# Linformer attention with a routed expert layer: W2's casts on other engines, batch 1's queries in other buffers, exponentials as steps of their own

## The chip, the cores and the metric

The kernel runs on one core of a Trainium2 chip. A core has five engines with queues of their own, each working strictly in the order of the program: TensorE (PE; the profile lists its weight loads apart, as PEld), VectorE (DVE), ScalarE (ACT), GpSimd (POOL) and SyncE (SP), which here only issues DMAs. The metric is the device time of one execution in microseconds (us); lower is better. A time that is called the median is that of several executions; the trace and the page come from one profiled execution, which has a time of its own.

## The reference, cut to what matters

Eight batches of 8 heads, 576 tokens, head width 64, 32 memory slots. All data are 32-bit floats.

```python
a = softmax(phi, axis=2)                              # [b, h, s, 32]
k_m = einsum('bhsm,bhsd->bhmd', a, k)                 # 32 keys and values a head
v_m = einsum('bhsm,bhsd->bhmd', a, v)
attn = softmax(q @ k_m.T / 8)                         # [b, h, s, 32]
x = (attn @ v_m) as [4608, 512]                       # heads side by side

logits = unit(x) @ unit(expert_emb).T / tau           # 8 experts
e = argmax(logits)                                    # one expert a token
gate = softmax(logits)[e]
out = gate * (relu(x @ w1[e]) @ w2[e])                # w1 [512, 1024], w2 [1024, 512]
```

The kernel computes the output of a batch with the expert that most of its tokens choose; tokens of other experts, if there are any, are done over at the end.

## The kernel before, in words

The heads lie in two groups of four (`g` = 0, 1). For a batch the work is:

- *Memory* (`softmax`, `turn`, `slots`, `block`, `flip`): exponentials of phi, its transposes, 32 keys and values per head. `block` scales them out of the accumulator `acc` (VectorE for the keys, line 427; ScalarE for the values, line 428), `flip` transposes them on TensorE (line 436) and ScalarE copies them out.
- *Scores* (`scores`, `Tokens.fill`, `weigh`, `divide`, `turn`): queries against the 32 keys on TensorE (line 453), copied to the buffer `sT` by ScalarE, and then per group a softmax over 32 values in `x`, [128, 576]: VectorE transposes (line 63), takes the maximum (line 70) and subtracts it (line 72), ScalarE takes the exponential (line 73), VectorE sums, divides (line 83) and transposes into `aw` (line 89).
- *Attention and routing* (`attend`, `norm`, `count`, `choose`, `late`): the rows of x with the logits, their lengths, the batch's expert. `choose` reads the expert into SyncE and issues the loads of that expert's W1, and for batches after the first those of W2.
- *Projection* (`project`, lines 531 to 535): the values times W1, in two halves of 512 columns, so that the first layer is one product of the attention weights `aT` with `gh` and `gl`. High and low parts (`...h`, `...l`) of a 32-bit number are kept apart, and a product is three products of such parts.
- *First layer* (`first`, lines 541 to 559): 2 halves of the tokens times 8 chunks of 128 columns, 16 chunks in all; six matmuls each (line 550) into one of four accumulators of the tag `mm`, drained by ScalarE's relu (line 553), VectorE's low part (line 554) and, in the second half, a second relu by ScalarE for the half tile (line 558).
- *Second layer* (`second`, lines 561 to 598): first the half tile, 64 tokens, straight from the 32-bit W2 in `w2s` (line 572); then four full tiles of 128 tokens. A full tile is 8 row blocks of W2 (`f` = 0 to 7), each three matmuls in the order `wh` with the high part, `wl` with the high part, `wh` with the low part (line 583). All five tiles end with a scaling by the gate (line 596) and an output DMA, which GpSimd issues.

The halves of W2 are made by `split_w` (line 514), one row block of 128x512 a call: a cast of `w2s` to `wh` by ScalarE (line 518), for blocks 1 and 5 by VectorE (line 520), then `wl` = `w2s` - `wh` by GpSimd (line 521).

The order on each engine is written by hand. `steps` builds two lists: what is issued behind each of the 16 chunks of the first layer (`first[0]` to `first[15]`) and behind each step of the second (`second[0]` to `second[7]` are the half tile, `second[8]` to `second[15]` the row blocks of the first full tile, and so on). These steps hold W2's split, the rest of this batch's routing and the preparation of the next batch `c` = b + 1 (`u`) and the memory part of b + 2. `batch` runs projection, first and second layer and calls the steps in between; `must(f)` sees that block f is split before a full tile reads it. So in batches 1 to 6 blocks 0 to 3 are split behind chunks 1, 3, 5 and 11 and blocks 4 to 7 behind steps 0, 2, 4 and 6 of the half tile, while both groups' `divide` and `turn` stand at `second[0]`. In batch 0 block 0 is split behind chunk 15 and the others in the half tile.

Loads are issued in order on SyncE's queue. Batch 0's queries and, from batch 2 on, all later ones come into `qt`. Batch 1's come into the front of `w2s`, so W2 of batch 0 is loaded only behind batch 1's scores, at `first[5]` of batch 0. Ahead of the batch loop, `moe_linformer` does the memory part and the scores of batch 0, chooses its expert from the first two of five token tiles, and prepares the memory of batch 1.

## Time and profile before

| | us |
|---|---|
| median of 3 runs | 508.51 (506.0 to 509.23) |
| the profiled execution | 506.96 |
| its span, first to last instruction | 505.0 |
| TensorE busy in it | 444.5 (88%) |
| VectorE, ScalarE, GpSimd busy | 275.4, 200.2, 133.0 |
| mean granted TensorE clock | 0.939 of full speed |

A row of a group names line, engine, operation, output and inputs, partitions x elements and how often; behind the bar stand busy time and mean ns of one, then how long the engine stood idle just ahead of these instructions and what ended that. A row in order of time begins with its start and its length in us from the start of the span. SPq rows are DMA issues on SyncE's queue. A row of stretches begins with the bounds in us. Matmuls overlap in the array and their ends are modelled, so the distance between two starts says more than a length does. The granted clock is 1.00 or 0.50 at any time; a mean lies between.

### The profile page before, as it was taken

The numbers are of one execution on the slowest core, as the hardware profiler recorded it, in microseconds if no ns is written. First come the engines' busy times: TensorE is split into PE (matmuls) and PEld (weight loads), VectorE is DVE, ScalarE is ACT, GpSimd is POOL, SyncE is SP. The second block draws the span as 40 slices with busy tenths as digits, with TensorE's granted clock in tenths as the row PEclk, the third lists the DMA queues.
The fourth block names the chain that finished last, engine by engine and source line by source line (L and its number), as shares of the span: only waits on it lengthen the run. The fifth ranks groups of instructions, "written<-read, shape, count | busy, mean of one in ns | idle before, by whom it ended". The sixth has DMA issues, their size and how long they took to land. (4 is left out here: it accounts for less than half of the span.)

```text
span 505.0 us, 9258 instructions
## 1 busy us (share of the span) xinstructions
PE 444.5 (88%) x3511; PEld 349.2 (69%) x3511; DVE 275.4 (55%) x854; ACT 200.2 (40%) x515; POOL 133.0 (26%) x132
## 2 busy tenths in 40 slices
PE   4679859999799997999799997999979998899994
PEld 3548537867587865868488684877758785688783
DVE  5675772746572675735745366726656367365300
ACT  3525423265233652246422463316522355115410
POOL 1020162222530324203333124303143032433400
PEclk9759969999799998999979999999979999899998
DMA  8962921694039800696018830298104800175011
GB/s 311 344 217 56 354 96 51 235 356 173 11 128 376 300 2 15 245 313 242 0 32 311 320 151 1 82 374 282 76 11 167 308 1 1 32 265 190 12 42 45
DMA packets 27585, 82.46 MB, mean 163 GB/s; under 512 B 7080, under 2 KB 7464, under 8 KB 25744
## 3 DMA queue, kind: packets, MB, share of 16 engines
q1 hardware_dynamic: 24736, 73.28, 40.9%
q0 software_dynamic: 2688, 8.26, 4.5%
q8 instruction: 29, 0.48, 0.4%
q10 hardware_dynamic: 112, 0.28, 0.2%
q14 instruction: 20, 0.16, 0.1%
HBM read 66.60 MB, written 15.20 MB: 162 GB/s over the span
## 5 line engine op out<-in xcount | busy, mean ns | idle before, releaser
L521 POOL TENSOR_TENSOR wl<-w2s,wh 128x512 fp32r<-128x512 f32 x64 | 85.5, 1349 | 178.0 <-ACT wh L518 109.9
L583 PE MATMUL py<-wh,hh 128*128 128x512 f32 x256 | 109.8, 429 | 16.9 <-DVE wh L520 15.5
L583 PE MATMUL py<-wl,hh 128*128 128x512 f32 x256 | 105.8, 413 | 9.7 <-POOL wl L521 9.7
L550 PE MATMUL ph<-aT,gh 128*128 128x288 f32 x512 | 106.9, 302 | 5.1 <-ACT h L558 4.8
L583 PE MATMUL py<-wh,hl 128*128 128x512 f32 x256 | 104.3, 407 | 0.0
L554 DVE SCALAR_TENSOR_TENSOR hl<-ph,hh 128x288 fp32r<-128x288 f32 x128 | 57.2, 454 | 60.1 <-ACT hh L553 60.1
L550 PEld LDWEIGHTS ph<-aT,gh 128*128 128x128 f32 x512 | 81.1, 188 | 11.4 <-ACT h L558 8.0
L550 PE MATMUL ph<-aT,gl 128*128 128x288 f32 x256 | 75.3, 294 | 0.0
L583 PEld LDWEIGHTS py<-wh,hh 128*128 128x128 f32 x256 | 50.2, 196 | 33.4 <-DVE wh L520 18.5
L583 PEld LDWEIGHTS py<-wl,hh 128*128 128x128 f32 x256 | 50.1, 196 | 25.6 <-POOL wl L521 17.5
L553 ACT ACTIVATE hh<-ph 128x288 fp32r<-128x288 f32 x128 | 51.8, 412 | 19.1 <-PE ph L550 19.1
L583 PEld LDWEIGHTS py<-wh,hl 128*128 128x128 f32 x256 | 50.5, 197 | 9.7
L596 ACT ACTIVATE ys<-py,gate 128x512 f32<-128x512 f32 (+1 forms) x39 | 25.0, 640 | 62.9 <-PE py L583 32.8
L550 PEld LDWEIGHTS ph<-aT,gl 128*128 128x128 f32 x256 | 48.0, 188 | 0.0
L534 DVE TENSOR_TENSOR gl<-pg,gh 128x512 fp32r<-128x512 f32 x32 | 19.9, 684 | 47.6 <-ACT gh L533 47.6
L687 POOL DMA_DIRECT2D out_dram<-ys x28 | 15.5, 552 | 107.2 <-ACT ys L596 40.8
L508 POOL TENSOR_TENSOR aT<-aw,aT 128x576 fp32r<-128x576 f32 (+2 forms) x18 | 23.1, 1301 | 61.9 <-DVE aT L507 61.9
L105 DVE TENSOR_REDUCE lg<-po 128x8 f32<-128x16 f32 x40 | 6.9, 174 | 50.8 <-PE po L100 50.8
L119 ACT COPY ea<-tt 128x512 f32<-128x512 f32 (+1 forms) x24 | 12.4, 515 | 55.8 <-PE tt L118 55.8
L572 PE MATMUL py<-w2s,h 128*64 128x256 f32 x256 | 30.5, 385 | 3.7 <-ACT h L558 3.7
L100 PEld LDWEIGHTS po<-vv,aw 128*128 128x128 f32 x160 | 28.9, 244 | 6.6 <-issue 3.2
L100 PE MATMUL po<-vv,aw 128*128 128x136 f32 x160 | 29.4, 336 | 3.4 <-DVE aw L89 3.4
(134 smaller groups left out, 535.2 us busy)
## 6 DMA issues: line engine op xcount, KB each, us to landing
kx<-kv SPq DMA_DIRECT2D x32, 512.0 KB, 6.9
w1s<-w SPq DMA_DIRECT2D x16, 1024.0 KB, 6.3
w2s<-w SPq DMA_DIRECT2D x32, 512.0 KB, 10.0
qt<-qT SPq DMA_DIRECT2D x14, 576.0 KB, 6.8
out_dram<-ys POOLq DMA_DIRECT2D x28, 256.0 KB, 5.5
ex<-phiT SPq DMA_DIRECT2D x16, 288.0 KB, 10.7
ad<-aw SPq DMA_DIRECT2D x8, 576.0 KB, 13.4
kl<-kvt SPq DMA_DIRECT2D x7, 256.0 KB, 3.8
```

What stands on the lines that cost most here:

```text
L100: nc.tensor.matmul(po[:, 144 * g : 144 * g + P + E], lhsT=k.aw[:, g, to], rhs=k.vv[:, g], start=True, stop=True)
L119: nc.scalar.copy(k.ea[:, ti[0] : ti[-1] + 1], t)
L508: self.nc.gpsimd.tensor_tensor(out=al, in0=a, in1=ah.bitcast(F32), op=ALU.subtract)
L521: nc.gpsimd.tensor_tensor(out=l, in0=x, in1=h.bitcast(F32), op=ALU.subtract)
L534: nc.vector.tensor_tensor(out=self.gl[:, g, f], in0=ps[g], in1=self.gh[:, g, f].bitcast(F32), op=ALU.subtract)
L550: nc.tensor.matmul(p, lhsT=w[:, g, fs], rhs=x[:, g, to], start=g == 0 and k == 0, stop=g == 1 and k == 2)
L553: nc.scalar.activation(self.hh[:, f, to], p, AF.Relu)
L554: nc.vector.scalar_tensor_tensor(out=self.hl[:, f, to], in0=p, scalar=0.0, in1=self.hh[:, f, to].bitcast(F32), op0=ALU.max, op1=ALU.subtract)
L572: nc.tensor.matmul(p[64 * j : 64 * j + 64], lhsT=self.h4[:, f], rhs=self.w2s[:, f, d * j : d * j + d], start=f == 0, stop=f == 7,)
L583: nc.tensor.matmul(p, lhsT=h[:, f, to], rhs=w[:, f], start=f == 0 and k == 0, stop=f == 7 and k == 2)
L596: nc.scalar.activation(y[:, :d], p, AF.Copy, scale=gate[:, i : i + 1])
L687: eng.dma_start(self.out[r : r + P], y)
```

## The change: what it does

- `split_w` takes the copy to use. In batches 1 to 7, blocks 0, 1 and 2 are cast and subtracted by GpSimd behind chunks 0, 3 and 6; blocks 3 to 7 are cast by ScalarE at steps 0, 1, 2, 4 and 5 of the half tile. In batch 0, ScalarE casts blocks 0 to 3 behind chunks 9, 11, 13 and 15 and blocks 4 to 7 at steps 0, 0, 1 and 1. VectorE casts none.
- Batch 1's queries go to `sT` (first half) and `x` (second half). The second half is loaded behind batch 0's use of `x`, and W2 of batch 0 right behind it, ahead of the batch loop.
- `weigh` has the exponential as a step of its own. The pieces of the two groups' softmax get new places, and `divide` and `turn` of group 1 go from `second[0]` to `second[3]` (batch 0: both from `second[0]`, to `second[4]` and `second[7]`).
- `flip` and `scores` of the next batch move one chunk later in batches 1 to 6; in batch 0, `slots(1, 1)` moves from behind the projection to chunk 2, with `block`, `flip` and `scores` after it at chunks 3, 5 and 7.
- `attend(2, 3)` and `norm(2, 3)` of batch 0 move from ahead of the batch loop to between the halves of its projection; five matmuls of ones into an accumulator that nobody reads stand ahead of the loop.
- `load_kv(2)` goes from chunk 5 to 3 and `load_q(2)` from chunk 5 to 12, behind `keep(0)`.

```diff
--- before.py
+++ after.py
@@ -70,6 +70,7 @@
         nc.vector.tensor_reduce(out=mx, in_=x, axis=AX.X, op=ALU.max)
         yield
         nc.vector.tensor_tensor(out=x, in0=x, in1=mx.unsqueeze(3).broadcast_to(x.shape), op=ALU.subtract)
+        yield
         nc.scalar.activation(x, x, AF.Exp, scale=1.0 / 8.0)
 
     def divide(self, gs, ks):
@@ -151,10 +152,9 @@
         nc.vector.tensor_scalar(
             out=k.seli[:, b : b + 1], in0=ki, scalar1=E - 1, scalar2=None, op0=ALU.bitwise_and
         )
-        self.e = nc.sync.value_load(k.seli[:, b : b + 1], min_val=0, max_val=E - 1)
-        k.load_w1(self.e, b == 0)
-        if b:
-            k.load_w2(self.e)
+        e = nc.sync.value_load(k.seli[:, b : b + 1], min_val=0, max_val=E - 1)
+        k.load_w1(e, b == 0)
+        return e
 
     def total(self):
         self.all = self.count(self.pt, "all", range(NT))
@@ -323,6 +323,13 @@
     def mm(self, shape, name):
         return self.ps.tile(shape, F32, tag="mm", name=name, bufs=4)
 
+    def warm(self, n):
+
+        hot = self.mm([P, 512], "hot")
+        x = self.ones.unsqueeze(1).broadcast_to((P, 4, P))
+        for _ in range(n):
+            self.nc.tensor.matmul(hot, lhsT=self.ones, rhs=x, start=True, stop=True)
+
 
     def load_phi(self, b, gs=range(NG)):
         if b < B:
@@ -337,12 +344,16 @@
 
     def load_q(self, b, halves=(0, 1)):
         if b < B:
-            for c in (slice(2 * k, 2 * k + 2) for k in halves):
-                self.nc.sync.dma_start(self.q(b)[:, c], self.qT[b, :, c])
-
-    def q(self, b):
-
-        return self.w2s[:, :5].rearrange("p c f -> p (c f)")[:, : NC * S].rearrange("p (c s) -> p c s", c=NC) if b == 1 else self.qt
+            for k in halves:
+                c = slice(2 * k, 2 * k + 2)
+                to = (self.sT, self.x.rearrange("p g k m -> p g (k m)"))[k] if b == 1 else self.qt[:, c]
+                self.nc.sync.dma_start(to, self.qT[b, :, c])
+
+    def q(self, b, c):
+
+        if b != 1:
+            return self.qt[:, c]
+        return self.sT[:, c] if c < 2 else self.x[:, c - 2].rearrange("p k m -> p (k m)")
 
     def load_w1(self, e, halves=False):
 
@@ -448,9 +459,8 @@
 
     def score(self, b, ts, lo, hi):
 
-        q = self.q(b)
         for g, j, r, c, i in self.heads():
-            self.nc.tensor.matmul(ts[g][j], lhsT=self.kT[r, c, i], rhs=q[r, c, lo:hi], start=True, stop=True)
+            self.nc.tensor.matmul(ts[g][j], lhsT=self.kT[r, c, i], rhs=self.q(b, c)[r, lo:hi], start=True, stop=True)
 
     def squares(self, b, ts):
 
@@ -511,14 +521,11 @@
         for g in range(NG):
             self.part(g, slice(0, S))
 
-    def split_w(self):
-        nc, j = self.nc, self.halves
+    def split_w(self, copy=None):
+        j = self.halves
         x, h, l = self.w2s[:, j], self.wh[:, j], self.wl[:, j]
-        if j % 4 != 1:
-            nc.scalar.copy(h, x)
-        else:
-            nc.vector.tensor_copy(out=h, in_=x)
-        nc.gpsimd.tensor_tensor(out=l, in0=x, in1=h.bitcast(F32), op=ALU.subtract)
+        (copy or self.nc.scalar.copy)(h, x)
+        self.nc.gpsimd.tensor_tensor(out=l, in0=x, in1=h.bitcast(F32), op=ALU.subtract)
         self.halves += 1
 
     def project(self, n, vT):
@@ -601,43 +608,45 @@
 
 
         first, second = ([[] for _ in range(n)] for n in (16, 40))
-        for f in (1, 3, 5, 11) if b else (15,):
+
+        for f in (0, 3, 6) if b else ():
+            first[f].append(lambda: self.split_w(self.nc.gpsimd.tensor_copy))
+        for f in () if b else (9, 11, 13, 15):
             first[f].append(self.split_w)
-        for n in (0, 2, 4, 6) if b else (0, 1, 2, 3, 4, 5, 7):
+        for n in (0, 1, 2, 4, 5) if b else (0, 0, 1, 1):
             second[n].append(self.split_w)
         if not b:
             late = t.late()
-            first[0].append(lambda: t.attend(4))
-            first[1].append(lambda: self.flip(1, 0))
-            first[1].append(lambda: t.norm(4))
-            first[2].append(t.total)
-            for f in (4, 6, 7, 9, 10, 12):
+            first[1] += [lambda: self.flip(1, 0), lambda: t.attend(4)]
+            first[2] += [lambda: t.norm(4), lambda: self.slots(1, 1)]
+            first[3] += [t.total, lambda: self.load_kv(2)]
+            for f in (5, 6, 8, 9, 11, 12):
                 first[f].append(lambda: next(late))
-            first[12] += [lambda: list(late), lambda: self.keep(0)]
+            first[12] += [lambda: list(late), lambda: self.keep(0), lambda: self.load_q(2)]
         if u:
-            c = b + 1
-            first[0].append(lambda: self.block(c, 1))
-            first[1 if b else 3].append(lambda: self.flip(c, 1))
-            first[3 if b else 5].append(lambda: self.scores(c))
+            c, o = b + 1, 0 if b else 3
+            first[0 + o].append(lambda: self.block(c, 1))
+            first[2 + o].append(lambda: self.flip(c, 1))
+            first[4 + o].append(lambda: self.scores(c))
+
+            places = (first[6], first[8], first[10], first[12]), (first[12], first[14], second[0], second[3])
             if not b:
-                first[5] += [lambda: self.load_w2(t.e), lambda: self.load_kv(2), lambda: self.load_q(2)]
+                places = (second[0], second[0], second[0], second[4]), (second[4], second[4], second[4], second[7])
             all = slice(0, BL)
             for g in range(NG):
                 work = u.weigh((g,), all)
-                pieces = [lambda g=g: u.fill((g,), all, [self.sT[:, i] for i in range(NG)])]
-                pieces += [lambda work=work: next(work, None)] * 2
-                for k, piece in enumerate(pieces):
-
-                    (first[6 * g + 2 * k + 5] if b else second[0]).append(piece)
-            for g in range(NG):
-                second[0].append(lambda g=g: (u.divide((g,), all), u.turn((g,), all)))
+                places[g][0].append(lambda g=g: u.fill((g,), all, [self.sT[:, i] for i in range(NG)]))
+                for at in places[g][1:]:
+                    at.append(lambda work=work: next(work, None))
+            for at, g in zip((second[0], second[3]) if b else (second[4], second[7]), range(NG)):
+                at.append(lambda g=g: (u.divide((g,), all), u.turn((g,), all)))
             o = 0 if b else 7
             second[14 + o].append(lambda: u.attend(0, 1, pt=self.mm))
             second[15 + o].append(lambda: u.norm(0, 1))
             second[16 + o].append(lambda: u.attend(2, 3))
             second[17 + o].append(lambda: u.norm(2, 3))
             second[18 + o].append(lambda: u.attend(4, pt=self.mm))
-            second[20 + o] += [u.choose, lambda: u.norm(4), self.parts, lambda: self.keep(c)]
+            second[20 + o] += [lambda: self.load_w2(u.choose()), lambda: u.norm(4), self.parts, lambda: self.keep(c)]
             second[21 + o] += [u.owner, u.flags]
             after = u.late()
             for n in (24, 25, 26, 28, 29, 30):
@@ -662,9 +671,11 @@
             while self.halves <= f:
                 self.split_w()
 
-        for _ in self.project(b, self.vT[b % 2]):
-            pass
-        if u:
+        for k, _ in enumerate(self.project(b, self.vT[b % 2])):
+            if not b and not k:
+                t.attend(2, 3)
+                t.norm(2, 3)
+        if b and u:
 
             self.slots(b + 1, 1)
         for n, _ in enumerate(self.first(b)):
@@ -849,8 +860,7 @@
     t.divide(range(NG), first)
     t.turn(range(NG), first)
     t.attend(0, 1, pt=k.mm, turned=False)
-    t.choose((0, 1))
-    k.load_q(1, (1,))
+    e = t.choose((0, 1))
     list(t.weigh(range(NG), others))
     for g in range(NG):
         k.part(g, slice(0, 256))
@@ -864,8 +874,9 @@
     t.norm(0, 1)
     k.block(1, 0)
     t.owner()
-    t.attend(2, 3)
-    t.norm(2, 3)
+    k.load_q(1, (1,))
+    k.load_w2(e)
+    k.warm(5)
     for b in range(B):
         u = Tokens(k, b + 1, k.pt) if b < B - 1 else None
         left = k.batch(b, t, u)
```

## The prediction

> **What bounds the kernel now.** I read the page first, then the stretches of each batch, the clock inside them, and last one batch's order of time. TensorE (PE) is the busy engine, and two of its groups carry nearly all of its named waits:
>
> ```profile
> span 505.0 us, 9258 instructions
> PE 444.5 (88%) x3511; PEld 349.2 (69%) x3511; DVE 275.4 (55%) x854; ACT 200.2 (40%) x515; POOL 133.0 (26%) x132
> L583 PE MATMUL py<-wh,hh 128*128 128x512 f32 x256 | 109.8, 429 | 16.9 <-DVE wh L520 15.5
> L583 PE MATMUL py<-wl,hh 128*128 128x512 f32 x256 | 105.8, 413 | 9.7 <-POOL wl L521 9.7
> ```
>
> So the second layer waits for the halves of W2: 15.5 us for VectorE's cast, 9.7 us for GpSimd's subtraction. The eight batches, cut where each projection starts (columns: length, then busy time of PE, PEld, DVE, ACT, POOL, then granted clock, DMA share, GB/s):
>
> ```profile
> 34.30:101.70 67.40, 59.16 (x455) 44.24 (x455) 39.93 (x136) 25.87 (x68) 16.76 (x15) 0.91 0.45 157
> 101.70:161.60 59.90, 55.02 (x446) 43.57 (x448) 33.85 (x103) 24.79 (x64) 16.77 (x16) 0.94 0.55 199
> 161.60:220.50 58.90, 53.75 (x439) 42.51 (x438) 33.77 (x103) 24.88 (x64) 16.80 (x16) 0.97 0.48 172
> 220.50:280.80 60.30, 55.16 (x447) 43.70 (x450) 33.86 (x103) 24.79 (x64) 16.80 (x16) 0.94 0.49 173
> 280.80:339.80 59.00, 53.86 (x439) 42.44 (x438) 33.77 (x103) 24.88 (x64) 16.78 (x16) 0.97 0.48 173
> 339.80:400.10 60.30, 55.19 (x445) 43.78 (x446) 33.86 (x103) 24.78 (x64) 16.80 (x16) 0.94 0.49 172
> 400.10:456.20 56.10, 50.93 (x387) 39.99 (x386) 31.34 (x94) 21.11 (x54) 16.77 (x16) 0.97 0.26 90
> 456.20:497.90 41.70, 41.06 (x257) 33.34 (x256) 10.65 (x24) 15.66 (x39) 10.70 (x9) 1.00 0.19 67
> ```
>
> Batches 1 to 6 each lose about 5 us of PE time, and also clock: 0.94 or 0.97. Batch 7, with no next batch to prepare, loses neither. One batch in order of time, where its second layer begins:
>
> ```profile
> 182.53 3.80 PE L572 MATMUL py<-w2s,h 128*64 128x256 f32 x32 [0.51 <-ACT h L558]
> 186.60 0.39 PE L583 MATMUL py<-wl,hh 128*128 128x512 f32 x1
> 189.58 0.40 PE L583 MATMUL py<-wh,hl 128*128 128x512 f32 x1
> 192.32 0.50 PE L583 MATMUL py<-wh,hh 128*128 128x512 f32 x1 [2.34 <-DVE wh L520]
> 193.76 0.79 PE L583 MATMUL py<-wl,hh 128*128 128x512 f32 x1 [0.94 <-POOL wl L521]
> ...
> 185.41 0.22 ACT L558 ACTIVATE h<-ph 128x64 f32<-128x64 f32 x1 [0.53 <-DVE hl L554]
> ...
> 187.25 0.76 DVE L83 TENSOR_TENSOR x<-x,z 128x576 f32<-128x576 f32 x1
> 190.19 0.76 DVE L83 TENSOR_TENSOR x<-x,z 128x576 f32<-128x576 f32 x1
> 191.88 0.38 DVE L520 CAST wh<-w2s 128x512 fp32r<-128x512 f32 x1
> ...
> 187.34 1.82 POOL L521 TENSOR_TENSOR wl<-w2s,wh 128x512 fp32r<-128x512 f32 x1 [4.57 <-ACT wh L518]
> 192.43 3.74 POOL L521 TENSOR_TENSOR wl<-w2s,wh 128x512 fp32r<-128x512 f32 x3 [3.27 <-DVE wh L520]
> ```
>
> VectorE casts the sixth row block (f = 5) only behind both groups' divisions and transposes, at 191.88; PE stands 2.34 us, then 0.94 us for GpSimd's half of that block. Then the clock:
>
> ```profile
> 60.65:64.06 3.41, 1.83 (x8) 0.97 (x6) 3.27 (x6) 0.68 (x1) 2.98 (x2) 1.00 1.01 406
> 190.35:193.77 3.42, 0.51 (x2) 0.20 (x2) 2.47 (x5) 0.81 (x2) 1.34 (x2) 1.00 0.00 0
> 193.77:197.18 3.41, 3.41 (x10) 2.81 (x11) 0.00 (x0) 0.06 (x1) 3.41 (x4) 0.50 0.00 0
> 238.14:241.55 3.41, 2.21 (x15) 1.69 (x14) 2.05 (x4) 1.88 (x7) 1.07 (x1) 1.00 0.00 0
> 241.55:245.32 3.77, 3.77 (x33) 2.16 (x33) 2.93 (x6) 1.75 (x7) 0.21 (x1) 1.00 0.00 0
> 475.80:497.90 22.10, 22.09 (x98) 17.85 (x96) 0.00 (x0) 3.33 (x6) 4.97 (x4) 1.00 0.12 42
> ```
>
> The stretch with the stall is followed by 3.41 us at half clock; a stretch with 2.21 us busy of 3.41 isn't; batch 7's unbroken second layer never is. So a stall is paid twice: while PE stands, and after it.
>
> **The change, part by part.** *Second layer, batches 1 to 6.* VectorE's casts go; GpSimd casts and subtracts blocks 0 to 2 during the first layer, ScalarE casts 3 to 7 as soon as the last relu is out (185.41 + 0.22 = 185.63, call it T). So PE no longer waits for VectorE. What is late next is GpSimd: five subtractions where three followed the late cast. Block 3's cast ends at T + 0.6, by one cast's 0.61:
>
> ```profile
> 180.81 0.61 ACT L518 CAST wh<-w2s 128x512 fp32r<-128x512 f32 x1
> 178.13 0.69 ACT L73 ACTIVATE x<-x 128x576 f32<-128x576 f32 x1 [0.44 <-DVE x L72]
> ...
> 167.12 0.44 PE L436 MATMUL tf_1True<-ident,kb 128*128 128x128 f32 x2 [0.59 <-DVE kb L427]
> 179.92 0.54 PE L550 MATMUL ph<-aT,gh 128*128 128x288 f32 x2 [0.70 <-ACT h L558]
> ...
> 475.73 5.04 POOL L521 TENSOR_TENSOR wl<-w2s,wh 128x512 fp32r<-128x512 f32 x4 [3.44 <-ACT wh L518]
> ...
> 1.45 0.95 POOL L290 MEMSET kl<- 64x1024 f32 x1
> ```
>
> Subtractions run 5.04 / 4 = 1.26 us apart, so the fifth ends at T + 0.6 + 6.3 = T + 6.9. A subtraction met by VectorE's multiplication L83 took 1.82 instead of about 1.26: two divisions fall into the five, +1.1, so T + 8.0. PE needs block f's low half at 186.60 plus f steps of three matmuls; from 186.60 to 189.58 thirteen matmuls pass, 0.229 each, 0.69 a step. Block 7 is due at 186.60 + 4.8 = 191.4 = T + 5.8. Stall left: 8.0 - 5.8 = 2.2 us, against 2.34 + 0.94 = 3.28. **Gain 1.1 x 6 = 6.5.** If no division collides it is 1.1 left (gain 2.2 each); if all five take 1.82, the end is T + 9.7, 3.9 left. I take two collisions because the two divisions stay in that stretch. ScalarE hides its casts beside the half tile's 3.80 us; group 1's exponential, now between casts, costs its 0.69 there, which GpSimd's lag covers.
>
> *Clock, batches 1 to 6.* Lost time is length times missing clock: three batches at 0.94 lose some 3.6 us, three at 0.97 some 1.8; PE was standing for part of the first, so I count 14.4 in all. The 2.2 us left come as three waits (before blocks 5, 6 and 7) over some 3.5 us. A 3.41 us stretch that holds all three would be busy about 1.7, below the 1.83 that still lost the clock in batch 0, and one that cuts off a wait would not. The stretches lie on a grid of their own; I reckon one batch in six, 1.7 us. **Gain 12.7.**
>
> *First layer, batches 1 to 6.* Three PE waits are in the quoted rows: 0.59 (the flip comes before the block's scaling is done), 0.70 and 0.51 (accumulators not yet drained). The flip moves one chunk later, more than 0.59. ScalarE's draining loses three casts of 0.61 and the 0.44 for which an exponential held it waiting for VectorE, more than 0.70 + 0.51. **Gain 1.80 x 6 = 10.8.** Bound below: 0.6 x 6 if draining still lags; above: 2.1 each.
>
> GpSimd's cast of a 128x512 block isn't in this trace. Lower bound the memory fill's rate, 0.95 us for 1024 elements, so about 0.5; upper, the two-input subtraction's 1.26. I take 1.0. Three casts and three subtractions are then 7 us, in the 24 us between the batch's start at 161.6 and T = 185.6, and nothing earlier waits on them: cost 0. Even at 4 us a cast, 16 us, they would fit; if they didn't, each us over would push all five later subtractions.
>
> *Batch 7.* No divisions, but five subtractions instead of four after T: its fourth ended at 480.77, just in time. A fifth ends 1.26 later: **loss 1.1**, less 0.4 from a first layer without casts on ScalarE.
>
> *Batch 0.* Its first full tile waits through this stretch:
>
> ```profile
> 60.60:78.00 17.40, 10.21 (x25) 5.46 (x24) 11.36 (x20) 4.31 (x8) 12.22 (x10) 0.71 0.37 137
> 34.34 3.10 PE L531 MATMUL pg<-w1s,vT 64*32 64x512 f32 x32
> 26.26 1.40 SPq L351 DMA_DIRECT2D w1s<-w  x2
> 46.91 2.07 SPq L357 DMA_DIRECT2D w2s<-w  x4
> DMA to landing us min/median/max: 7.6/7.6/7.6
> ```
>
> Seven blocks were cast after the first layer; now four are, and the fill, maximum and subtraction of the softmax are spread. The tile's 24 matmuls need 24 x 0.229 = 5.5; with 2.2 of stall, 7.7 instead of 17.4: gain 9.7. Against it: three more casts of 0.61 in its first layer, between 0 and 1.8 as draining hides them or not, I take 1.3; and one half-clock stretch of 1.7 at even odds, 0.9. **Gain 7.5** with the rest at nothing. That rest: attend(2,3) moves behind the first half projection, which can start no earlier than W1's landing (the last row: 26.26 + 7.6 = 33.9, against 34.34 now), so the order changes and the work doesn't; the five matmuls of ones run where PE waits for W1, and can at best bring full clock into the 3.10 us of the projection (half of that, 1.5); slots(1,1) moves into the first layer. I bound all this at -1.5 to +1.5. On SP's queue the second half of batch 1's queries now waits for x, behind it stand W2's four loads; they go out once the transposes of batch 0 are done, ahead of the projection at 34.34 instead of at 46.91, and the first reader is the cast in chunk 9 of 16, ten us after the projection. Cover gone, a late W2 would cost batch 0 its lateness, once. load_kv(2) goes earlier and load_q(2) later by a few us, both first needed in or before batch 1: nothing.
>
> **Sum.** 6.5 + 12.7 + 10.8 - 0.7 + 7.5 = 36.8. The profiled execution took 506.96 for its span of 505.0; 506.96 - 36.8 = 470.2. The median of the runs is 1.55 above the profiled one, so 472.
>
> **Rivals.** *The clock drop stays* (0.18): the three remaining waits trip it in every batch. Six stretches of at least 3.41 at half clock cost 1.7 each, 10.2, or the whole 14.4; instead of the 1.7 counted: 472 + 8.5 to 12.7, about 483. For it: GpSimd's shortfall stays in the same place. Against it: 2.2 us in three pieces, and the stretch with 2.21 busy. The Trainium skill, "TensorE: Matmul & The Clock Gate", section "HAM oscillation", says the clock falls only for PE gaps above some 3.4 us. By that rule the 2.34 us stall isn't what takes the clock, the drop has another cause and stays, and the time is this rival's 483. The trace disagrees: gaps of 2.34 and 0.94 us are followed by 0.50, and the one batch without them keeps 1.00.
>
> *GpSimd becomes the bound* (0.07): all five subtractions blocked, 3.9 us stall and the clock lost: the 6.5 turns to -3.7, the 12.7 to nothing, batch 0 loses 3 more: 472 + 10 + 13 + 3 = 498. For it: 1.82 was seen. Against: that one stands beside an L83, and batch 7's four, with no division near, kept 1.26.
>
> *Slower* (0.05): GpSimd's cast is slow. Place: the first layer. The chain 3 x (c + 1.26) starts with the batch at 161.6 and must end by T - 1.8 = 183.8; these 22.2 us allow c = 6.1. From there each us of c costs 3 us in seven batches, and the clock's 12.7 as well; at c = 8, 5.7 x 7 = 40: 472 + 53 = 525. It is slower by over 1% from c = 7.5 on (4.2 x 7 + 12.7 = 42). Against: both bounds, 0.5 and 1.26, are far from it.
>
> **How the numbers follow.** My forecast has 0.70: with its own bounds (stall 1.1 to 3, first layer 0.6 to 2.1, batch 0 by 3) 463 to 480. The range takes in the clock rival: 463 to 487. A difference of 1% is what a measurement of this kernel can tell from none, 5 us. Faster by more: all but the slow cast and about a third of the GpSimd rival, plus a little for what I haven't seen, 0.90; within 1%, 0.05; slower, 0.05.
>
> **What would show it.** Right: no PE wait on a VectorE cast; waits on GpSimd's low half before blocks 5 to 7 of about 2 us a batch; clock 0.98 or more in batches 1 to 6; no waits of 0.59 and 0.70 in the first layer; second layer of batch 7 with a new wait of about 1 us; batch 0 near 60 us. Wrong: the clock at 0.94 to 0.97 still; a GpSimd cast above 4 us; batch 0's projection starting later than 35 us.

## The result, and the profile after

The changed kernel takes 472.72 us (median; 471.92 to 473.85), the kernel before beside it on the same chip 508.62: a ratio of 0.9305 [0.9266, 0.9344], 7.0% faster. The forecast was 472. The profiled execution took 472.12 us, at a mean granted clock of 0.979 (0.939 before).

The page after: the span with the busy times, and the three groups of PE that matter.

```profile
span 470.2 us, 9244 instructions
PE 428.2 (91%) x3516; PEld 337.7 (72%) x3516; DVE 287.0 (61%) x838; ACT 196.5 (42%) x510; POOL 145.1 (31%) x153
L590 PE MATMUL py<-wl,hh 128*128 128x512 f32 x256 | 102.6, 401 | 6.0 <-POOL wl L528 5.7
L590 PE MATMUL py<-wh,hh 128*128 128x512 f32 x256 | 105.7, 413 | 0.0
L101 PE MATMUL po<-vv,aw 128*128 128x136 f32 x160 | 26.0, 298 | 11.7 <-DVE aw L90 11.7
```

The 15.5 us for VectorE's cast are gone, 9.7 us for GpSimd's half have become 5.7. In their place stands a group that the prediction didn't speak of: the next batch's attention (line 101) waits 11.7 us for VectorE's transposes. The stretches of the eight batches, cut at the same places as before (bounds, length, busy time of PE, PEld, DVE, ACT, POOL, granted clock, DMA share, GB/s):

```profile
32.47:93.44 60.97, 57.60 (x466) 44.63 (x466) 42.78 (x143) 27.24 (x71) 17.99 (x17) 0.97 0.53 187
93.44:148.22 54.78, 51.92 (x439) 41.23 (x439) 35.57 (x101) 24.06 (x63) 18.51 (x19) 1.00 0.62 217
148.22:202.96 54.74, 51.83 (x439) 41.23 (x439) 35.57 (x101) 24.06 (x63) 18.53 (x19) 1.00 0.52 187
202.96:257.94 54.98, 51.88 (x439) 41.24 (x439) 35.78 (x101) 24.18 (x63) 18.49 (x19) 1.00 0.53 187
257.94:314.61 56.67, 53.42 (x439) 42.55 (x438) 35.65 (x101) 24.16 (x63) 18.53 (x19) 0.97 0.50 181
314.61:369.35 54.74, 51.87 (x440) 41.24 (x439) 35.56 (x101) 24.06 (x63) 18.49 (x19) 1.00 0.53 189
369.35:421.02 51.67, 48.80 (x386) 38.84 (x385) 33.27 (x92) 20.41 (x53) 18.49 (x19) 1.00 0.28 96
421.02:463.43 42.41, 41.34 (x257) 33.05 (x256) 9.99 (x22) 15.38 (x38) 12.43 (x12) 1.00 0.19 68
```

Everything up to batch 1's projection became 8.26 us shorter (101.70 to 93.44), batches 1 to 6 together 26.9 (354.5 to 327.58), batch 7 became 0.7 longer and the tail behind it 0.3 shorter: 34.8, the whole difference of the spans. Five of the six batches keep full clock, batch 4 does not.

Batch 2 in order of time, where its second layer begins: PE's waits, and what ScalarE, VectorE and GpSimd do meanwhile.

```profile
170.28 0.65 PE L579 MATMUL py<-w2s,h 128*64 128x256 f32 x4 [0.40 <-ACT h L565]
175.18 0.50 PE L590 MATMUL py<-wl,hh 128*128 128x512 f32 x1 [0.39 <-POOL wl L528]
176.43 0.50 PE L590 MATMUL py<-wl,hh 128*128 128x512 f32 x1 [0.29 <-POOL wl L528]
179.16 0.96 PE L101 MATMUL po<-vv,aw 128*128 128x136 f32 x6 [1.77 <-DVE aw L90]
...
170.00 0.22 ACT L565 ACTIVATE h<-ph 128x64 f32<-128x64 f32 x1 [0.53 <-DVE hl L561]
170.81 6.79 POOL L528 TENSOR_TENSOR wl<-w2s,wh 128x512 fp32r<-128x512 f32 x5 [15.06 <-ACT wh L527]
171.33 0.82 DVE L82 TENSOR_SCALAR z<-z 128x18 f32<-128x18 f32 x1
172.48 1.50 DVE L84 TENSOR_TENSOR x<-x,z 128x576 f32<-128x576 f32 x1
174.90 0.71 DVE L81 TENSOR_REDUCE z<-x 128x18 f32<-128x576 f32 x1
175.65 0.77 DVE L82 TENSOR_SCALAR z<-z 128x18 f32<-128x18 f32 x1
176.75 1.47 DVE L84 TENSOR_TENSOR x<-x,z 128x576 f32<-128x576 f32 x1
178.32 0.78 DVE L90 STREAM_TRANSPOSE aw<-x 128x576 f32<-128x576 f32 x1
```

GpSimd starts its five subtractions 0.6 us behind the last relu (170.22), as predicted, and runs them in 6.79 us, near the 6.3 of an undisturbed chain: four of the five take 1.26 to 1.31 us each, the third 1.81. It is VectorE that is held: the division's multiplication (line 84) takes 1.50 and 1.47 us instead of 0.76, and line 82, which handles only 18 elements, about 0.8 us instead of 0.18 (its undisturbed length stands in the run "all by GpSimd" below). So group 1's transposes end late and PE stands 1.77 us in the attention. ScalarE's casts aren't what holds VectorE: ScalarE stands idle from 173.8 to 179.9, and the second multiplication, from 176.75 on, takes 1.47 us all the same.

Two pairs of neighbouring stretches on the clock's grid, the first pair from batch 2, the second from batch 4:

```profile
177.26:180.67 3.41, 1.64 (x14) 1.47 (x13) 3.02 (x9) 0.77 (x2) 1.37 (x3) 1.00 0.18 38
180.67:184.09 3.42, 3.42 (x23) 3.02 (x22) 2.24 (x11) 2.60 (x7) 0.57 (x1) 1.00 0.00 0
286.48:289.90 3.42, 1.30 (x9) 1.05 (x8) 2.96 (x5) 0.00 (x0) 1.86 (x3) 1.00 0.19 41
289.90:293.31 3.41, 3.41 (x13) 2.92 (x12) 2.06 (x10) 2.88 (x6) 0.00 (x0) 0.50 0.00 0
```

The wait in the attention lies across a bound of the grid or inside one stretch, as it happens: with 1.64 us busy the clock stayed, with 1.30 it fell to 0.50 for the next 3.41 us.

### The profile page after: what moved, and what is told of

Its sections match the earlier page's. It is cut to its first block, busy times and chain, and to the rows that moved or that the text cites. A ratio compares the mean times of both kernels' runs of the same rounds, so it can differ in the third digit from the quotient of the medians.

```text
span 470.2 us, 9244 instructions
## 1 busy us (share of the span) xinstructions
PE 428.2 (91%) x3516; PEld 337.7 (72%) x3516; DVE 287.0 (61%) x838; ACT 196.5 (42%) x510; POOL 145.1 (31%) x153
## 3 DMA queue, kind: packets, MB, share of 16 engines
q0 software_dynamic: 2688, 8.26, 4.9%
## 5 line engine op out<-in xcount | busy, mean ns | idle before, releaser
L590 PE MATMUL py<-wl,hh 128*128 128x512 f32 x256 | 102.6, 401 | 6.0 <-POOL wl L528 5.7
L557 PE MATMUL ph<-aT,gh 128*128 128x288 f32 x512 | 105.3, 300 | 1.0 <-DVE gl L541 0.5
L590 PE MATMUL py<-wh,hh 128*128 128x512 f32 x256 | 105.7, 413 | 0.0
L590 PE MATMUL py<-wh,hl 128*128 128x512 f32 x256 | 100.6, 393 | 0.0
L590 PEld LDWEIGHTS py<-wh,hh 128*128 128x128 f32 x256 | 48.4, 189 | 12.7 <-issue 3.9
L590 PEld LDWEIGHTS py<-wh,hl 128*128 128x128 f32 x256 | 48.4, 189 | 10.1
L698 POOL DMA_DIRECT2D out_dram<-ys x28 | 15.5, 553 | 110.7 <-ACT ys L603 71.3
L101 PE MATMUL po<-vv,aw 128*128 128x136 f32 x160 | 26.0, 298 | 11.7 <-DVE aw L90 11.7
L101 PEld LDWEIGHTS po<-vv,aw 128*128 128x128 f32 x160 | 23.7, 201 | 16.0 <-DVE aw L90 13.4
L565 ACT ACTIVATE h<-ph 128x64 f32<-128x64 f32 x64 | 14.3, 224 | 34.3 <-DVE hl L561 34.3
L579 PEld LDWEIGHTS py<-w2s,h 128*64 128x64 f32 x256 | 16.3, 136 | 16.6 <-ACT h L565 10.7
```

Source lines behind the costliest of these rows:

```text
L101: nc.tensor.matmul(po[:, 144 * g : 144 * g + P + E], lhsT=k.aw[:, g, to], rhs=k.vv[:, g], start=True, stop=True)
L557: nc.tensor.matmul(p, lhsT=w[:, g, fs], rhs=x[:, g, to], start=g == 0 and k == 0, stop=g == 1 and k == 2)
L565: nc.scalar.activation(self.h4[:, f], p[:, HS - 64 :], AF.Relu)
L579: nc.tensor.matmul(p[64 * j : 64 * j + 64], lhsT=self.h4[:, f], rhs=self.w2s[:, f, d * j : d * j + d], start=f == 0, stop=f == 7,)
L590: nc.tensor.matmul(p, lhsT=h[:, f, to], rhs=w[:, f], start=f == 0 and k == 0, stop=f == 7 and k == 2)
L698: eng.dma_start(self.out[r : r + P], y)
```

## The experiments

Batches 1 to 6 repeat from one to the next, while the end of the old batch 0 varies between executions of the same code by up to some 4 us (in three runs with the old batch 0 it ended at 104.8 to 105.7 instead of 101.70, with a lower clock). The new batch 0 is steadier: from its projection to batch 1's it takes 60.96 to 61.00 us in five runs that have it (59.45 in a sixth, which kept full clock), and only its start moves, between 32.47 and 33.19. So beside the ratio against the kernel before, which each run was timed with, I compare batches 1 to 6 as one stretch, from batch 1's projection to batch 7's. The two ends of that comparison, first before, then after:

```profile
101.70:456.19 354.49, 323.91 (x2575) 255.98 (x2575) 200.44 (x609) 145.23 (x374) 100.72 (x96) 0.96 0.46 164
```

```profile
93.44:421.02 327.58, 309.72 (x2576) 246.32 (x2575) 211.40 (x597) 140.93 (x368) 111.03 (x114) 0.99 0.50 177
```

### The stall filled, nothing else

The kernel before, with twelve matmuls of ones ahead of the row block for which PE waits; `warm` is the change's own function.

```diff
+            if b and u:
+                second[12].append(lambda: self.warm(12))
```

> The kernel before, with twelve matmuls of ones (128x512, into an accumulator that nobody reads) queued on TensorE ahead of row block 5 in batches 1 to 6, where it stands 2.34 us for VectorE's cast. The output is not touched. Theory 'the stall takes the clock': the wait is still there but the array works through most of it, so the 0.50 stretches behind it go; batches 1 to 6 lose some 14.4 us of half clock and gain at most 0.3 us each of extra work: about 508.6 - 12 = 496, granted clock 0.97 or more. Rival 'the clock drop has another cause, the stall is not what takes it' (the rule of the Trainium skill, TensorE: Matmul & The Clock Gate, that only gaps above some 3.4 us do, leads here too): the 0.50 stretches stay where they are, and the time is 508.6 to 511.

Measured: 499.78 us, ratio 0.9815 [0.9755, 0.9875]. Batches 1 to 6 as one, and then the place of the stall in batch 2 in order of time:

```profile
104.91:449.43 344.52, 326.06 (x2648) 251.81 (x2647) 200.22 (x609) 145.68 (x374) 100.88 (x96) 1.00 0.47 169
```

```profile
191.13 2.76 PE L332 MATMUL hot<-ones 128*128 128x512 bf16 x12
193.61 0.52 PE L591 MATMUL py<-wh,hh 128*128 128x512 f32 x1
195.05 0.50 PE L591 MATMUL py<-wl,hh 128*128 128x512 f32 x1 [0.93 <-POOL wl L529]
```

VectorE's cast is as late as before. From the last matmul of W2 ahead of the ones to the first behind them it is 193.61 - 190.89 = 2.72 us between starts, and 192.32 - 189.58 = 2.74 where PE stood; the 0.93 behind them is still there. Yet batches 1 to 6 are 10.0 us shorter, at a clock of 1.00 throughout. So the clock's share is shown by itself: the stall takes as long filled as idle, and without the half-clock stretches behind it 10.0 us go, fewer than the 14.4 that I had counted. Some of their cost is hidden in the kernel before: at full clock PE comes sooner to the next block's low half and stands for it, 0.28 us at 196.29 in this batch, a wait that the half clock had covered. The Trainium skill, "TensorE: Matmul & The Clock Gate", section "HAM oscillation", gives the rule "no PE-idle gaps >~3.4µs"; that shorter gaps do no harm is how the prediction read it. These runs show that they do: the gaps were 2.34 and 0.94 us, and filling the first brought the clock back.

### Only the casts of W2

The kernel before with the new engines and places of the casts in batches 1 to 7; divisions, exponentials, queries and batch 0 as they were. The lines by which `split_w` takes the engine are left out here.

```diff
...
-        for f in (1, 3, 5, 11) if b else (15,):
+        for f in (0, 3, 6) if b else ():
+            first[f].append(lambda: self.split_w(nc.gpsimd.tensor_copy))
+        for f in () if b else (15,):
             first[f].append(self.split_w)
-        for n in (0, 2, 4, 6) if b else (0, 1, 2, 3, 4, 5, 7):
+        for n in (0, 1, 2, 4, 5) if b else (0, 1, 2, 3, 4, 5, 7):
```

> The kernel before, with only W2's casts of batches 1 to 7 as in the changed kernel (blocks 0 to 2 by GpSimd in the first layer, 3 to 7 by ScalarE in the half tile); exponentials, divisions, staging and batch 0 as before. Theory 'the engine of the cast is what counts': the wait on VectorE goes, as does most of the clock loss; per batch 3.3 less stall, 2.1 less clock, about 0.8 in the first layer, against a GpSimd chain of 0.7 and a new wait for VectorE's transposes of up to 1.8: about 4 x 6 = 24, to 485. Rival 'the order on VectorE is what counts' (the division of group 1 standing ahead of the cast): little is gained without the new places, 500 to 508.

Measured: 486.68 us, ratio 0.9566 [0.9514, 0.9619]. Batches 1 to 6 as one, and PE's waits of batch 2:

```profile
104.77:436.98 332.21, 313.67 (x2576) 244.58 (x2575) 203.60 (x597) 143.91 (x368) 113.94 (x114) 1.00 0.50 175
```

```profile
166.22 0.44 PE L436 MATMUL tf_1True<-ident,kb 128*128 128x128 f32 x2 [0.59 <-DVE kb L427]
179.02 0.53 PE L549 MATMUL ph<-aT,gh 128*128 128x288 f32 x2 [0.70 <-ACT h L557]
...
192.03 0.50 PE L582 MATMUL py<-wl,hh 128*128 128x512 f32 x1 [0.78 <-POOL wl L520]
```

22.3 of the 26.9 us come with the casts alone: no wait on a VectorE cast, and full clock. But the first layer keeps its waits of 0.59 and 0.70; the casts' new places removed only the 0.51 ahead of the half tile.

### Only the order on VectorE

The kernel before with one edit: group 1's division and transposes behind step 3 instead of step 0. VectorE still casts blocks 1 and 5.

```diff
-                second[0].append(lambda g=g: (u.divide((g,), all), u.turn((g,), all)))
+                second[3 if b and g else 0].append(lambda g=g: (u.divide((g,), all), u.turn((g,), all)))
```

> The kernel before, with one edit: in batches 1 to 7 the division and transposes of group 1 are issued at step 3 of the half tile instead of step 0, so that VectorE's cast of block 5 (step 2) stands ahead of them. No cast changes engine. Theory 'either alone removes the wait' (the cast off VectorE, or the second division behind it): the cast runs at 189.0 on the old clock of batch 2 and is due at 190.0; no wait on VectorE, about 0.9 us of waits on low halves stay, no half-clock stretch: (3.3 - 0.9 + 1.8) x 6 = 25, so 482 to 486, level with the run that moved only the casts (486.7). Rival 'the division's delay is passed on': the attention of the next batch waits for group 1's transposes instead, by 1 to 2 us a batch: 488 to 494. Rival 'the engine counts': 505 or more.

Measured: 487.60 us, ratio 0.9567 [0.9523, 0.9611]. Batches 1 to 6 as one, and batch 2 in order of time, VectorE's cast and PE's waits:

```profile
105.71:438.34 332.63, 312.07 (x2575) 245.58 (x2574) 208.52 (x609) 145.09 (x374) 103.89 (x96) 1.00 0.49 175
```

```profile
189.06 0.52 DVE L520 CAST wh<-w2s 128x512 fp32r<-128x512 f32 x1
191.07 0.50 PE L583 MATMUL py<-wl,hh 128*128 128x512 f32 x1 [0.76 <-POOL wl L521]
193.80 0.96 PE L100 MATMUL po<-vv,aw 128*128 128x136 f32 x6 [0.54 <-DVE aw L89]
```

The same gain as from all the casts (332.63 and 332.21 us; the ratios are alike to 0.0001). Counted from the start of the half tile, the cast comes 2.95 us earlier (189.06 - 182.66 = 6.40, where before 191.88 - 182.53 = 9.35), because one group's division, not two, stands ahead of it. What VectorE does late instead is group 1's transposes, and 0.54 us of that shows in the attention: the rival's wait, smaller than it said, which leaves the time 1.6 us above the theory's range. So either edit alone removes the stall on the cast, and with both, the second is worth little, as the next run shows.

### The changed kernel with the old casts

The other half of the same question: everything of the change but the casts' engines and places in batches 1 to 7 (`split_w` gives blocks 1 and 5 to VectorE again; its lines are left out here).

```diff
...
-        for f in (0, 3, 6) if b else ():
-            first[f].append(lambda: self.split_w(self.nc.gpsimd.tensor_copy))
-        for f in () if b else (9, 11, 13, 15):
+        for f in (1, 3, 5, 11) if b else (9, 11, 13, 15):
             first[f].append(self.split_w)
-        for n in (0, 1, 2, 4, 5) if b else (0, 0, 1, 1):
+        for n in (0, 2, 4, 6) if b else (0, 0, 1, 1):
```

> The changed kernel, with W2's casts of batches 1 to 7 as before (blocks 1 and 5 by VectorE, blocks 0 to 3 in the first layer, 4 to 7 at steps 0, 2, 4, 6). Theory 'the engine of the cast is what counts': the cast of block 5 again stands on VectorE behind a division and a transpose, and the wait, the clock loss and the first layer's casts come back: 6 x 4 = 24 more, about 497. Rival 'the order on VectorE is what counts': the cast now stands behind group 0's division alone, at about 3.9 us after the last relu, and is due at about 4.3: no wait on VectorE, clock kept, 473 to 479 with the three casts on ScalarE in the first layer.

Measured: 474.27 us, ratio 0.9334 [0.9285, 0.9383], within the interval of the changed kernel. Batches 1 to 6:

```profile
92.59:422.36 329.77, 313.76 (x2575) 246.71 (x2575) 211.76 (x609) 142.81 (x374) 100.78 (x96) 0.99 0.50 176
```

2.2 us more than after, 0.4 a batch, with one half-clock stretch in each of the two. With the rest of the change in place, the part that gives the change its name is worth hardly more than a measurement can tell.

### Exponentials and divisions at their old places

The changed kernel, with each exponential directly behind its subtraction and both divisions at step 0.

```diff
-            places = (first[6], first[8], first[10], first[12]), (first[12], first[14], second[0], second[3])
+            places = (first[6], first[8], first[10], first[10]), (first[12], first[14], second[0], second[0])
...
-            for at, g in zip((second[0], second[3]) if b else (second[4], second[7]), range(NG)):
+            for at, g in zip((second[0], second[0]) if b else (second[4], second[7]), range(NG)):
```

> The changed kernel, with the exponentials of batches 1 to 6 issued right behind the subtraction again (chunk 10 and step 0) and both divisions at step 0. Theory 'the new places hardly matter once the cast is off VectorE': ScalarE waits some 0.3 us for VectorE at step 0, GpSimd's chain moves by as much, VectorE's own order is unchanged: 472 to 477. Rival 'the exponentials' places carry part of the gain': ScalarE's casts of blocks 4 to 7 are held, the low halves come 1 us later and the clock drops in some batches: 480 to 488.

Measured: 479.67 us, ratio 0.9442 [0.9391, 0.9493]. Batches 1 to 6 as one, and the waits of batch 2:

```profile
93.59:427.74 334.15, 314.16 (x2575) 250.08 (x2574) 211.53 (x597) 141.80 (x368) 111.18 (x114) 0.98 0.49 174
```

```profile
165.54 0.69 ACT L74 ACTIVATE x<-x 128x576 f32<-128x576 f32 x1 [0.44 <-DVE x L72]
167.33 0.54 PE L557 MATMUL ph<-aT,gh 128*128 128x288 f32 x2 [0.73 <-ACT h L565]
180.41 1.52 PE L101 MATMUL po<-vv,aw 128*128 128x136 f32 x6 [1.77 <-DVE aw L90]
```

6.6 us more in batches 1 to 6. The chain is in two rows: ScalarE waits 0.44 us for VectorE's subtraction, drains the accumulators that much later, and PE stands 0.73 us. So it was the exponentials' places, not the lighter ScalarE, that removed the 0.70 of the first layer; three half-clock stretches also came where after has one. The attention's wait is the same 1.77 with both divisions at step 0: so it doesn't come from the new place of group 1's division. What it does come from, the next run tells.

### All eight blocks by GpSimd, in the first layer

This takes the suspected collision away. In the changed kernel, GpSimd is idle for 15 us of each first layer (the row of 170.81 above). Here it casts and subtracts all eight blocks there, and nothing of W2's split is left beside the divisions.

```diff
-        for f in (0, 3, 6) if b else ():
+        for f in (0, 2, 4, 6, 8, 10, 12, 14) if b else ():
             first[f].append(lambda: self.split_w(self.nc.gpsimd.tensor_copy))
...
-        for n in (0, 1, 2, 4, 5) if b else (0, 0, 1, 1):
+        for n in () if b else (0, 0, 1, 1):
```

> The changed kernel, with all eight blocks of W2 cast and subtracted by GpSimd in the first layer of batches 1 to 7 (chunks 0, 2, 4 ... 14), none in the half tile. At 0.61 and about 1.36 us a block the chain is 16 us and ends with the first layer. Theory 'GpSimd's five late subtractions hold VectorE, and VectorE is late for the attention': the two multiplications of the division fall from 1.5 to 0.76 us and the small operation between from 0.8 to 0.2, the transposes end some 2.7 us sooner, the new wait of 1.77 us of TensorE and the two waits on low halves (0.6 together) go: 2.4 x 6 + 0.7 in batch 7 + the clock of batch 4, so 456 to 459. Rival 'VectorE is late by its own work, or by the exponential': the 1.77 us stay, only the 0.6 go: 468 to 470. If the subtraction of the maximum inside the first layer is now held instead, the first layer grows by up to 0.7 a batch, and 461.

Measured: 453.52 us, ratio 0.8921 [0.8878, 0.8965]. Batches 1 to 6 as one, and batch 2 in order of time, the divisions and the attention:

```profile
94.16:403.83 309.67, 304.68 (x2576) 245.94 (x2575) 194.90 (x597) 125.80 (x338) 129.49 (x144) 1.00 0.53 187
```

```profile
161.38 0.61 POOL L527 CAST wh<-w2s 128x512 fp32r<-128x512 f32 x1
162.06 1.88 POOL L528 TENSOR_TENSOR wl<-w2s,wh 128x512 fp32r<-128x512 f32 x1
...
172.25 0.18 DVE L82 TENSOR_SCALAR z<-z 128x18 f32<-128x18 f32 x1
172.76 0.76 DVE L84 TENSOR_TENSOR x<-x,z 128x576 f32<-128x576 f32 x1
174.45 0.96 PE L101 MATMUL po<-vv,aw 128*128 128x136 f32 x6 [0.30 <-DVE aw L90]
```

Lines 82 and 84 are back at 0.18 and 0.76 us, the attention waits 0.30 instead of 1.77, no low half is waited for in this batch, the clock is 1.00. That settles the collision: same divisions in the same place, GpSimd's chain gone from beside them. (ScalarE's five casts have gone from there too, but the second multiplication was held while ScalarE stood idle.) The time is 2.5 us below the 456 to 459 that I expected. The last subtraction of the first layer shows the collision from the other side: it meets VectorE's two-input subtraction and takes 1.88 us where the other seven take 1.27 to 1.30. Batches 1 to 6 lose 17.9 us (327.58 to 309.67). The named waits give 0.39 + 0.29 + 1.77 - 0.30 = 2.15 a batch, 12.9, and batch 4's clock 1.9, which leaves 3.1. But waits are counted from modelled ends. By starts, batch 2 takes 8.30 us from its first full tile to the end of the attention's wait after the change (170.86 to 179.16) and 5.61 here (168.84 to 174.45): six times 2.69 makes 16.1, and with the 1.9 that is all of it.

### The attention later

The rival remedy: leave GpSimd and VectorE as they are and let PE ask later. The attention of the next batch moves by three, two and one steps, and `norm` behind it with it (left out here).

```diff
+            lag = 3 if b else 0
-            second[14 + o].append(lambda: u.attend(0, 1, pt=self.mm))
+            second[14 + o + lag].append(lambda: u.attend(0, 1, pt=self.mm))
...
-            second[16 + o].append(lambda: u.attend(2, 3))
+            second[16 + o + (lag and 2)].append(lambda: u.attend(2, 3))
...
-            second[18 + o].append(lambda: u.attend(4, pt=self.mm))
+            second[18 + o + (lag and 1)].append(lambda: u.attend(4, pt=self.mm))
```

> The changed kernel, with the attention of the next batch issued later in the second layer in batches 1 to 6 (first pair of tiles three steps, the second pair two, the last one step later). Theory 'TensorE's new wait is its place in the order, nothing waits on the result': the 1.77 us go and nothing comes in their place: 1.8 x 6 = 10.6 and the half-clock stretch of batch 4, so 460 to 462. Rival 'the result is needed soon': the expert's choice, the split of the attention weights and the loads of W1 and W2 slip by some 1.4 us and the next projection waits: 468 to 473.

Measured: 466.35 us, ratio 0.9169 [0.9122, 0.9216]. Batches 1 to 6 as one, and what batch 2 waits for instead:

```profile
94.14:415.33 321.19, 309.55 (x2575) 244.72 (x2574) 209.57 (x597) 140.25 (x368) 111.11 (x114) 1.00 0.51 180
```

```profile
177.63 0.50 PE L590 MATMUL py<-wl,hh 128*128 128x512 f32 x1 [0.28 <-POOL wl L528]
...
186.05 0.17 PE L141 MATMUL key<-oh,ones 128*128 128x8 bf16 x1 [0.56 <-DVE oh L109]
```

6.4 us less, where the 1.77 alone would be 10.6. Block 7's low half is late as well (0.28): the attention had stood ahead of it and hidden that. And the count of the experts, which stayed in its place, now comes 0.56 us too soon after the attention. 1.77 - 0.28 - 0.56 = 0.93 a batch would be 5.6. By the lengths of the batches the gain is less in most: 0.64 to 0.72 us in batches 1, 2, 3 and 5, 1.46 in batch 6, and 2.20 in batch 4, where the kept clock is part of it. The time lies between the ranges of the two theories, and both were partly right: the wait goes, and about half of it comes back elsewhere.

### Both remedies

All eight blocks by GpSimd, and the first pair of the attention one step later.

```diff
+            k = 1 if b else 0
-            second[14 + o].append(lambda: u.attend(0, 1, pt=self.mm))
-            second[15 + o].append(lambda: u.norm(0, 1))
+            second[14 + o + k].append(lambda: u.attend(0, 1, pt=self.mm))
+            second[15 + o + k].append(lambda: u.norm(0, 1))
```

> The run with all eight blocks by GpSimd, with the first pair of the next batch's attention one step (three matmuls, 0.69 us) later in batches 1 to 6. That run still shows 0.3 us of TensorE waiting for VectorE's transposes there. Theory: these 0.3 x 6 = 1.8 go and nothing comes in their place: 451 to 452.5 against 453.5. Rival 'the expert's choice behind it is then waited for', as 0.56 us a batch were in the run that moved the attention by three steps: 453 to 455.

Measured: 452.08 us (451.27 to 453.07), ratio 0.8878 [0.8849, 0.8908]; batches 1 to 6 take 308.75 us. The 0.30 of the attention is gone, and a wait of the next transposes for ScalarE (0.31 us in batch 2) has come. In the profiles 0.9 us is left of the 1.8 that six times 0.30 would give, and 1.4 between the medians; the intervals of the two ratios overlap. Its median is the lowest of all versions run, but that it is faster than the run with the first remedy alone isn't shown. By the ratios to the kernel before it stands at 0.8878 / 0.9305 = 0.954 of the changed kernel.

### The matmuls of ones left out

```diff
-    k.warm(5)
```

> The changed kernel without the five matmuls of ones ahead of the batch loop. Theory 'they do nothing that lasts': the profile has them end at 30.6, then TensorE waits 1.85 us for W1, and the clock that they brought falls back to 0.50 at 33.9 to 37.3: between 1 us slower and 1 faster, 472 to 474. Rival 'they carry the start of batch 0': the projection runs at half clock throughout and batch 0 starts 1.5 to 3 us later, 474 to 476.

Measured: 473.49 us, ratio 0.9318 [0.9273, 0.9364]. The same as the changed kernel within the intervals. The profile tells more. The clock is 0.50 from 30.00 to 37.90, so the first half of the projection runs at half clock, as the rival says: it takes 1.96 us instead of 1.09. From the projection to batch 1's (33.24 to 94.79) it is 61.55 us, while five runs with the ones have 60.96 to 61.00. So the ones are worth some 0.6 us there, less than the rival's 1.5 to 3, and a median of this kernel doesn't resolve it. With the ones, the first half of batch 0's projection stands so:

```profile
32.47 1.09 PE L538 MATMUL pg<-w1s,vT 64*32 64x512 f32 x16 [1.85 <-DMA w1s<-w]
```

### The queries back in W2's buffer

The changed kernel, with batch 1's queries in the front of `w2s` as before, and W2 of batch 0 loaded behind the scores that read them.

```diff
-                to = (self.sT, self.x.rearrange("p g k m -> p g (k m)"))[k] if b == 1 else self.qt[:, c]
-                self.nc.sync.dma_start(to, self.qT[b, :, c])
+                self.nc.sync.dma_start((self.stage() if b == 1 else self.qt)[:, c], self.qT[b, :, c])
...
+            if not b:
+                first[7].append(lambda: self.load_w2(self.e0))
...
```

> The changed kernel, with batch 1's queries in the buffer of W2 again and W2 of batch 0 loaded behind batch 1's scores (chunk 7 of batch 0); all else as changed. Theory 'the staging is what lets batch 0 split early': W2 is issued near 50 and lands 5 to 10 us later, ScalarE's cast behind chunk 9 stands waiting for it and holds the draining of the first layer: batch 0 takes 4 to 9 us more, 477 to 482. Rival 'W2 lands in time anyway': 472 to 474.

Measured: 473.07 us, ratio 0.9326 [0.9273, 0.9379]. Batch 0 in order of time, where the first casts of W2 stand:

```profile
54.69 0.62 ACT L530 CAST wh<-w2s 128x512 fp32r<-128x512 f32 x1 [1.94 <-DMA w2s<-w]
56.42 0.77 PE L560 MATMUL ph<-aT,gh 128*128 128x288 f32 x2 [2.52 <-ACT h L568]
```

W2 lands too late: ScalarE stands 1.94 us in front of the cast, cannot drain meanwhile, and PE stands 2.52. From its projection to batch 1's, batch 0 takes 63.06 us (32.24 to 95.30) instead of 60.97. The total doesn't show these 2.1 us, since in this execution batch 4 kept its clock (batches 1 to 6 took 325.32). So the staging does its work as the theory says, but it is worth less than the 4 to 9 us expected, and a median of this kernel doesn't resolve it.

## Why the prediction was right, point by point

The time was right, 472 against 472.72, and its main line held: a stall paid twice, a lighter first layer, a shorter batch 0. Of its terms some were off, and one mechanism was misplaced.

- **The stall.** Predicted 1.1 us a batch gained, 2.2 left; measured 0.83 gained (3.28 before; 0.39 + 0.29 + 1.77 = 2.45 after). The size is near, but the step "a subtraction met by VectorE's multiplication L83 took 1.82 instead of about 1.26: two divisions fall into the five" had the wrong party paying. GpSimd's chain kept nearly its pace (one of its five subtractions took 1.81), and VectorE's lines 82 and 84 took 0.6 to 0.75 us more each, four times. From there the lateness went to the transposes and the attention, a reader that the prediction had not followed. Block 7, which it took for the measure of what is left, waited not at all, because the attention stands ahead of it. The low halves alone cost 0.68 us, not 2.2; that the total came out near is chance.
- **What ended the stall.** The prediction credited the casts' leaving VectorE. They do end it (casts only: 332.21), but so does the new place of group 1's division (order only: 332.63), and with that place kept, the casts are worth 2.2 us (casts back). It treated the divisions' place only as a source of collisions. The sum came out right because the two overlap.
- **The clock.** One batch of six was to drop, and one did, with some luck: the prediction reckoned it from three waits on low halves, while the wait that takes the clock is the attention's, and with the same code from batch 1 on none dropped in another execution (queries back in W2's buffer). The term was too large: 12.7 predicted. By batch 2's halves, below, the clock's share is 26.9 - 6 x (2.06 + 0.83) = 9.6 us, plus 1.9 lost again in batch 4 (56.67 against 54.74), so 11.5 for all of it; filling the stall gave 10.0. The step that was off is "length times missing clock", 14.4. One reason is seen in the filled stall: at full clock PE waits 0.28 us for a low half that comes in time at half clock. Whether that is the whole difference is not shown.
- **The first layer.** Predicted 1.80 a batch, measured 2.06 in batch 2: from the end of the projection to the last matmul of the half tile 21.65 us before (164.68 to 186.33), 19.59 after (151.34 to 170.93). Its waits of 0.59, 0.70 and 0.51 are gone, and a 0.40 is left in the half tile. But the step "ScalarE's draining loses three casts of 0.61 and the 0.44 ... more than 0.70 + 0.51" put two causes together: the casts took the 0.51 (casts only), the exponentials' places the 0.70 (exponentials back). The 0.59 also stays with casts alone and is gone where flip comes a chunk later, as predicted.
- **GpSimd's cast.** Taken as 1.0 us between bounds of 0.5 and 1.26; it took 0.61, as long as ScalarE's. Hidden, as said.
- **Batch 7.** A loss of 0.7 predicted, 0.7 measured (41.70 to 42.41), and by its parts: 1.1 of new waits were predicted, and from the first full tile to the end of the batch it takes 23.35 us (440.08 to 463.43) instead of 22.12 (475.78 to 497.90), 1.2 more; the rest of the batch is 0.5 shorter, where 0.4 was predicted.
- **Batch 0.** Predicted 7.5, measured 8.26, of which 1.83 is an earlier first projection (34.30 to 32.47), which the prediction had bounded at 1.5 and set at nothing. Its step "can start no earlier than W1's landing", 33.9, was wrong. W1 comes in two loads, of which the first half of the projection needs one, and PE's wait for it ends 5.9 us after the first issue at 26.53 (32.47 in the row shown with the matmuls of ones). Against the three other executions of the old batch 0 (104.8 to 105.7) the gain would be 11 to 12 us, so that the size came near owes something to the execution that was profiled.
- **The sum.** Of batches 1 to 6 the prediction had 30.0 and got 26.9: 1.5 less from the stall, 3.1 less from the clock, 1.6 more from the first layer. Batch 0 gave 0.8 and the tail 0.3 more. The profiled executions differ by 34.8, not 36.8. That the median still came to 472 owes something to chance: I had carried 1.55 from the profiled time to the median, and after it is 0.6.
- **The rivals.** "The clock drop stays" fell with the rows of 1.00. "GpSimd becomes the bound" and the slow cast fell with 6.79 for five subtractions and 0.61 for a cast. The collision of the second was real, only on the other engine, and taking it away was worth 17.9 us in batches 1 to 6, batch 4's clock among them (all by GpSimd).

## What to carry to other kernels

When an instruction waits for an engine that works in order, look first at what stands ahead of the producer on that engine: moving one division by three steps did as much as taking the work off the engine. A stall of the matmul engine should be priced with the clock that it takes after it, and a few dummy matmuls in the stall are a quick test of that share. In this kernel GpSimd's two-input work is best placed where VectorE has little two-input work of its own, even if GpSimd then has to do the casts as well: a cast takes GpSimd 0.61 us and VectorE 0.38, yet the version with the lowest median gives GpSimd every block from batch 1 on.

## What the runs showed of the hardware

In these traces GpSimd's subtraction and VectorE's two-input operations don't run side by side: one of them is held, and it is the one that began later. A subtraction of GpSimd that began 0.02 us behind VectorE's two-input subtraction (all by GpSimd, 162.06 and 162.04) went from 1.29 to 1.88 us; in the changed kernel, with a subtraction under way, VectorE's multiplication went from 0.76 to 1.50 and line 82's operation on 18 elements from 0.18 to 0.82 (it ends at 172.15, 0.04 us behind the subtraction that was under way), while the reduction (0.71) and the transposes (0.78) in the same stretch kept their times. The Trainium skill, "GPSIMD Engine Reference", section "Key points", says that GpSimd shares its ways into SBUF with VectorE, with contention where VectorE has two inputs in SBUF or runs in a mode with two ports. The multiplication, the subtraction and the reduction agree with it; whether line 82 runs in such a mode no run here shows, and that section has no sizes.

The clock's fall has no sharp bound in these profiles. Of stretches of 3.41 us, one with 1.64 us of modelled PE time kept the clock and one with 1.30 lost it; but the prediction's rows have one with 1.83 that lost it, the run without the ones has one with 1.64 that lost it (177.82 to 181.23), and the run with the old casts one with 2.16 (174.83 to 178.24). So the busy time of a stretch, as modelled here, doesn't decide by itself.
